# A fused attention and gated FFN kernel: instruction order from a stored table, FFN halves of 287 and 289 tokens, last output tile in two column halves

## The chip, the cores and the metric

The kernel runs on one core of a Trainium2 chip. The metric is the device time of one execution in microseconds; the median of several runs is compared. An execution is a little longer than the span from its first to its last instruction, which is what the profile shows.

## The reference

There are 8 batches, 8 heads, 576 tokens and a head width of 64, all in float32. The weights of the FFN come as float64 (`moe_w_in` 512 x 1024, `moe_conv_w` 3 x 1024, `moe_w_out` 1024 x 512), and the kernel decodes them from their two 32-bit words on the chip.

```python
scores = scale * np.matmul(q, k.transpose(0, 1, 3, 2))
mask = block_i >= block_j                      # blocks of 64 tokens
scores = np.where(mask, scores, -1000000000.0)
scores = scores - np.max(scores, axis=-1, keepdims=True)
attn = np.exp(scores)
attn = attn / (np.sum(attn, axis=-1, keepdims=True) + 1e-09)
x = (attn @ v).transpose(0, 2, 1, 3).reshape(B, S, H * D)
h = np.maximum(x @ w_in, 0.0)
conv_out = sum(conv_w[k] * hp[:, k:k + S] for k in range(3))   # hp: h with one zero token at each end
gate = 1.0 / (1.0 + np.exp(-conv_out))
return h * gate @ w_out
```

A token's gate needs the FFN's hidden value of the token before it and the one after it. A part of the tokens therefore needs one more column of `h` at each inner border.

## The kernel before, in words

**Precision.** TensorE works on 32-bit values in a reduced form. Each factor is split into a high and a low part, and products are sums of three matmuls: high by high, high by low, low by high. The parts are `wih`, `wil` for w_in, `woh`, `wol` for w_out, `xs[c][0]`, `xs[c][1]` for the attention's output, `gbuf[0]`, `gbuf[1]` for the gated hidden values.

**Attention.** Heads go in pairs, 4 pairs to a batch. For a pair, the q and k tiles are transposed on TensorE (`naturals`, L1020), evicted by ACT and DVE into high and low parts, and copied by DMA into stacked tiles (`mvz` L1057, `mv` L1077). `stage_s` computes scores block by block (L1227, L1229, L1182), DVE takes the maximum (L1237), ACT the exponential (L1240), POOL scales by the reciprocal sum (L1156). `stage_x` transposes the probabilities (L1418) and splits them by ACT and DVE (L1429, L1432, L1438). `stage_pv` multiplies them with v (L1516). `to_x` converts the pair's output on POOL to high and low parts (L675 and L1692), which the FFN reads.

**FFN.** `ffn(b, o0, o1, ...)` takes tokens o0 to o1 of a batch. For each of 8 blocks of 128 hidden units, 12 matmuls (4 chunks of 128 input features, 3 passes; L1598) fill one bank of PSUM, six planner operations of two matmuls each. ACT, DVE and POOL then apply the ReLU, the three taps of the convolution, the gate and the split (L1612 to L1638). For each output tile of 128 tokens, 24 matmuls of 512 columns follow (8 blocks, 3 passes; L1657), an eviction by ACT (L1667) and a store (L1670). Batch 0 goes in two parts, tokens 0 to 254 after a first round of attention over 256 tokens ("A") and the rest after a second round ("B"). Batches 1 to 7 go in two halves of 288 tokens. A half computes 290 columns: two more at the inner border, of which one is used. Tokens that don't fill an output tile are carried to the next part.

**Weights.** w_in comes in 8 blocks (`load_w_in`, block 0 in two halves), w_out in 8 (`load_w_out`, DMA L972). `split` and `decode` work on each: ACT takes the absolute value (L817), POOL or DVE clamps (L823; the tuple `S2P` lists the blocks that POOL clamps), DVE shifts and joins words (L828 to L851), ACT writes the high part (L886). The low part is made in a bank: minus the high part (L902), plus the low word's share (L905). For the blocks in the tuple `WPA`, a full-precision matmul also adds the value itself (L911) and ACT copies the result (L914); for the others DVE adds the value while it reads the bank (L908).

**Order.** The kernel isn't written in the order in which it runs. Each piece of work is handed to a planner as an operation with an engine, a duration, what it depends on, buffers and a due time (`Plan.op`). When all are known, `Plan.order` plans the whole program: `forward` goes through time, at each step takes the engine that can start first, and on it the ready operation with the earliest due time; FFN matmuls are marked `paced`, and are held back until they come within `WINDOW` (19.66 us) of the first attention operation not yet started. `late` then plans backwards to give new due times, and the two are repeated `ROUNDS` (24) times; the plan that ends first is kept. The resulting sequence on each engine is fixed in the program. DMA loads and stores are issued by SyncE (SP), one queue in order. The planner knows durations by formula (`c_act`, `c_dve`, `c_pool`, `mm_`), transfer times (`xfer`), a port that DVE and POOL share, the 8 banks of PSUM, and a clock of TensorE that falls after little use. In gaps of TensorE that it foresees, it puts dummy matmuls (`work`, L1808).

Of the kernel before, what the change touches and what calls it, by code (L numbers as in the profile page):

```python
# [18 lines left out]
PE, DVE, ACT, POOL, SP = 0, 1, 2, 3, 4  # L19

# [72 lines left out]
class Plan:  # L93
# [53 lines left out]

    def late(self, done):  # L150
        ops = self.ops
        top = max(o.end for o in ops)
        left = [0] * len(ops)
        for o in ops:
            for d in o.deps + o.after:
                left[d.seq] += 1
        rt = [0.0] * len(ops)
        free, port = [0.0] * 5, 0.0
        ready, future = [[] for _ in range(5)], [[] for _ in range(5)]
        for o in ops:  # L160
            if not left[o.seq]:
                heapq.heappush(future[o.eng], (0.0, top - o.end, o.seq, o))
        n = len(ops)
        res = [0.0] * n
        while n:
            best = None
            for e in range(5):
                t = free[e]
                while future[e] and future[e][0][0] <= t:
                    o = heapq.heappop(future[e])[3]  # L170
                    heapq.heappush(ready[e], (top - o.end, o.seq, o))
                if ready[e]:
                    p, _, o = ready[e][0]
                    cand = (max(t, port) if o.port else t, p, e, o, 0)
                elif future[e]:
                    t, p, _, o = future[e][0]
                    cand = (max(t, port) if o.port else t, p, e, o, 1)
                else:
                    continue
                if best is None or cand[:2] < best[:2]:  # L180
                    best = cand
            t, _, e, o, where = best
            heapq.heappop(future[e] if where else ready[e])
            end = t + (o.end - o.start)
            free[e] = end
            if o.port:
                port = end
            res[o.seq] = end
            n -= 1
            for d in o.deps + o.after:  # L190
                lat = self.DRAIN[d.eng] + (self.SIGNAL[e] if d.eng != e else 0.0) if (d.eng != PE or e != PE) else 0.0
                rt[d.seq] = max(rt[d.seq], end + d.lat + lat)
                left[d.seq] -= 1
                if not left[d.seq]:
                    heapq.heappush(future[d.eng], (rt[d.seq], top - d.end, d.seq, d))
        return [top - r for r in res]

    def order(self, window, skip, fill, clock, rounds, pair):
        best, least = None, 1e30
        for _ in range(rounds + 1):  # L200
            done = self.forward(window, skip, fill, clock, pair)
            if done is None:
                break
            end = max(o.end for o in self.ops)
            if end < least:
                best, least = done, end
                slots = [(b, b.slot) for q in self.queue.values() for b in q]
            for o, t in zip(self.ops, self.late(done)):
                o.target = t
            window = 1e9  # L210
        for b, z in slots:
            b.slot = z
        return best

    def forward(self, window, skip, fill, clock, pair):
# [22 lines left out]

        n = len(slots)
# [34 lines left out]
        front = sorted((o for o in self.ops if o.eng == PE and not o.paced), key=lambda o: (o.target, o.seq))  # L274
        fpos = 0
# [4 lines left out]
        open_, force = [], False  # L280
# [13 lines left out]
        while left:  # L294
            left -= 1
            best = None
            while fpos < len(front) and front[fpos].start is not None:
                fpos += 1
            limit = front[fpos].target + window if fpos < len(front) else 1e30
            for e in range(5):  # L300
                t = free[e]
                if e == PE:
# [3 lines left out]
                    for o in open_:  # L306
                        if o.paced and o.target > limit and not force:
                            continue
# [38 lines left out]
                if best is None or cand[:2] < best[:2]:  # L347
                    best = cand
            if best is None:
                if force:  # L350
                    return None
                force = True
                left += 1
                continue
            force = False
# [77 lines left out]
def kernel(  # L433
# [19 lines left out]
    HS = S // 2  # L453
    SCALE = 1.0 / 8.0
# [41 lines left out]
    S2P = tuple(range(16))  # L496
# [8 lines left out]
    WPA = (0, 1, 2, 3)  # L505
# [4 lines left out]
    WINDOW = 19.66  # L510
    ROUNDS = 24
# [136 lines left out]
    def c_pool(n, two_in=False):  # L648
        return 0.1 + n * 0.0022 if two_in else 0.16 + n / 1200.0
# [28 lines left out]
    def load_nat(p, at, part=None):  # L678
# [3 lines left out]
        for z, src in enumerate((q, k)):  # L682
# [10 lines left out]
            res.append((n, pl.op(SP, 1.5, go, at, bufs=ns[0:z + 1], xfer=c_dma(2 * (S - P * c0) * D * 4, 256))))  # L693
# [7 lines left out]
    def load_v(p, at, part, load_at=None):  # L701
# [11 lines left out]
        ld = pl.op(SP, 2.4, go, at if load_at is None else load_at, bufs=[vn], xfer=c_dma(2 * 5 * P * D * 4, 256))  # L713
# [99 lines left out]
    def decode(parts, scratch, deps, bufs, at, low=None, pool=False):  # L813
        fin, clamp = [], []
        for j, (words, n) in enumerate(parts):
# [3 lines left out]
            clamp.append(pl.op(ACT, c_act(n, False), s1, at, deps=deps, bufs=bufs))  # L819
# [12 lines left out]
        if pool:  # L832
            o3 = pl.op(POOL, c_pool(tot), s2, at, deps=clamp, bufs=bufs)
# [3 lines left out]
        for j, (words, n) in enumerate(parts):  # L837
# [19 lines left out]
            o4 = pl.op(DVE, c_dve(n), s4, at, deps=[o3], bufs=bufs, port=True)  # L857
            o = pl.op(DVE, c_dve(n, True), s5, at, deps=[o4], bufs=bufs, port=True)
            o = pl.op(DVE, c_dve(n), s6, at, deps=[o], bufs=bufs, port=True)
# [9 lines left out]
    def split(f, parts, src, hi, lo, scratch, deps, bufs, at, go, share=1):  # L869
# [51 lines left out]
        else:  # L921
            o1 = pl.op(ACT, c_act(n_), fh, at + 1, deps=[x[0] for x in o], bufs=bufs)
# [117 lines left out]
    def stage_t(nat, at):  # L1040
# [10 lines left out]
        for which in range(2):  # L1051
            t0 = at + 2.0 * which
            es = both[which]
            if which == 0:
                for o_, z, f_, n in ((0, 0, 0, S), (64, S + 64, 0, S - 64), (64, S, S - 64, 64)):
# [4 lines left out]
                    o = pl.op(SP, 0.65, mvz, t0 + (1.6 if n > 64 else 4.5), deps=es[0::2], bufs=[qh, t["qz"]], xfer=c_dma(n * 256, 2048))  # L1060
# [12 lines left out]
            for dst, o_, src, f_ in moves:  # L1073
# [5 lines left out]
                ready[dst in ("qb", "kb")].append(pl.op(SP, 0.65, mv, t0 + 1.5, deps=need, bufs=[src, t[dst]], xfer=c_dma(S * 256, 2048)))  # L1079
# [765 lines left out]
```

## Time and profile before

| what | value |
|---|---|
| time, median of 3 runs (lowest, highest) | 771.57 us (770.54, 771.87) |
| the profiled execution | 771.25 us |
| its span, first to last instruction | 769.5 us |
| mean granted TensorE clock | 0.996 |
| instructions | 17039 |
| busy share of PE, DVE, ACT, POOL | 98%, 82%, 80%, 57% |
| read from and written to HBM | 38.30 MB, 9.44 MB |

PE is TensorE's matmuls, PEld its weight loads, which overlap them; SPq is SyncE's queue of DMA issues. A matmul's end is modelled and its tail lies over the next one's start, so a stretch in which PE is busy all the time can still hold short delays between starts. A line such as L1598 is a line of the kernel before.

### The profile page before, as it was taken

The page shows a single profiled execution, that of the slowest core. Times are in us where ns is not written, and L with a number is a line of the kernel's source. Part 1 is how long each engine was busy: PE and PEld are TensorE (multiplying, and loading weights), DVE is VectorE, ACT ScalarE, POOL GpSimd, SP SyncE. Part 2 cuts the span into 40 slices and gives each one's busy share as a digit, 9 for nine tenths or more (in the row PEclk, how much of TensorE's full clock was granted, in tenths as well). Part 3 has the DMA queues.
Part 4 walks back from the last instruction along what each step waited for, and adds up shares of the span by engine and source line. Part 5 has one row for each costly group of instructions (what it writes and reads, how often), then busy time and mean ns, then how long its engine had stood idle before and what let it go on. Part 6 is the DMA issues. An engine that isn't in the chain of part 4 may idle for free.

```text
span 769.5 us, 17039 instructions
## 1 busy us (share of the span) xinstructions
PE 752.4 (98%) x5245; PEld 678.1 (88%) x5245; DVE 633.1 (82%) x1849; ACT 614.4 (80%) x1780; POOL 440.2 (57%) x664
## 2 busy tenths in 40 slices
PE   8889999999999999999999999999999999999998
PEld 5668879888989899998989889898999889898996
DVE  5898979988979879798988879798898888896540
ACT  5999978977979779797978879797887868786761
POOL 4556665676565557557565656557566643665421
PEclk9999999999999999999999999999999999999999
DMA  9823574567554554455455554555456363530001
GB/s 258 222 66 93 144 180 111 126 150 165 120 125 118 141 139 115 108 137 134 102 134 135 122 133 105 123 129 140 109 140 143 83 145 100 133 88 14 15 29 42
DMA packets 165839, 92.66 MB, mean 120 GB/s; under 512 B 135516, under 2 KB 142196, under 8 KB 165748
## 3 DMA queue, kind: packets, MB, share of 16 engines
q1 hardware_dynamic: 165204, 91.43, 48.9%
q8 instruction: 43, 0.70, 0.4%
q14 instruction: 48, 0.39, 0.2%
q10 hardware_dynamic: 544, 0.13, 0.1%
HBM read 38.30 MB, written 9.44 MB: 62 GB/s over the span
## 4 chain that ended last, share of the span: by engine, by line
PE 84%; ACT 6%; DVE 5%; DMA 2%; issue 1%; POOL 1%; SPq 0%; ACTq 0%; DVEq 0%
PE bank L1657 25%; PE bank L1598 25%; PE bank L1516 12%; PE bank L1418 6%; PE bank L1227 4%; PE bank L1229 4%; PE bank L1182 3%; PE bank L1020 2%; DMA ptbh<-in_k_dram 1%; DMA x<-in_moe_w_out_dram 1%; DVE ptbl L1432 1%; DVE st L1237 1%; DVE t L1619 1%; ACT ptbh L1429 1%; DVE xt L1539 1%
## 5 line engine op out<-in xcount | busy, mean ns | idle before, releaser
L1598 PE MATMUL bank<-x,wih 128*128 128x290 f32 (+2 forms) x1024 | 183.3, 300 | 1.5 <-ACT ptbl L1438 1.1
L1638 POOL TENSOR_TENSOR gl<-t,gh 128x288 fp32r<-128x288 f32 (+2 forms) x128 | 103.5, 812 | 108.8 <-ACT gh L1635 105.8
L1598 PEld LDWEIGHTS bank<-x,wih 128*128 128x128 f32 x1024 | 151.8, 189 | 4.5 <-ACT ptbl L1438 1.2
L1657 PE MATMUL bank<-woh,gh 128*128 128x512 f32 x288 | 117.1, 407 | 0.0
L1657 PE MATMUL bank<-woh,gl 128*128 128x512 f32 x288 | 113.6, 395 | 0.0
L1657 PE MATMUL bank<-wol,gh 128*128 128x512 f32 x288 | 113.5, 394 | 0.0
L1237 DVE TENSOR_REDUCE st<-bank 128x1 f32<-128x128 f32 (+1 forms) x224 | 106.5, 480 | 2.6
L1429 ACT ACTIVATE ptbh<-bank 128x384 fp32r<-128x384 f32 (+2 forms) x192 | 94.1, 504 | 14.9 <-PE bank L1418 14.2
L1432 DVE TENSOR_TENSOR ptbl<-bank,ptbh 128x512 fp32r<-128x512 f32 (+1 forms) x144 | 90.6, 632 | 6.6 <-ACT ptbh L1429 4.9
L1598 PE MATMUL bank<-x,wil 128*128 128x290 f32 (+2 forms) x512 | 94.3, 298 | 0.0
L1619 DVE SCALAR_TENSOR_TENSOR t<-bank,cw,t 128x288 f32<-128x288 f32 (+3 forms) x128 | 64.7, 506 | 23.2 <-ACT t L1615 21.7
L1598 PEld LDWEIGHTS bank<-x,wil 128*128 128x128 f32 x512 | 76.9, 189 | 0.5
L675 POOL TENSOR_SCALAR vv<-vn 128x320 fp32r<-128x320 f32 (+2 forms) x68 | 30.7, 454 | 73.5 <-PE bank L1516 43.0
L1229 PE MATMUL bank<-kl,qz 128*128 128x128 f32 (+1 forms) x224 | 72.3, 324 | 0.0
L1516 PE MATMUL bank<-ptbl,vv 128*64 128x320 f32 (+1 forms) x256 | 67.8, 313 | 0.0
L1615 ACT ACTIVATE t<-bank,cw 128x288 f32<-128x288 f32 (+2 forms) x128 | 63.9, 500 | 2.9 <-POOL gl L1638 0.8
L1623 DVE SCALAR_TENSOR_TENSOR t<-bank,cw,t 128x287 f32<-128x287 f32 (+3 forms) x128 | 64.6, 505 | 1.3
L1657 PEld LDWEIGHTS bank<-woh,gl 128*128 128x128 f32 x288 | 54.0, 188 | 12.8
L1635 ACT ACTIVATE gh<-t 128x288 fp32r<-128x288 f32 (+2 forms) x128 | 56.6, 445 | 8.8 <-DVE t L1631 8.6
L1628 ACT ACTIVATE t<-t 128x288 f32<-128x288 f32 (+2 forms) x128 | 56.8, 444 | 8.5 <-DVE t L1623 7.6
L1631 DVE SCALAR_TENSOR_TENSOR t<-t,bank 128x288 f32<-128x288 f32 (+2 forms) x128 | 56.8, 445 | 6.9 <-ACT t L1628 5.7
L1539 DVE TENSOR_TENSOR xt<-bank,xt 64x256 f32<-64x256 f32 (+1 forms) x112 | 51.5, 460 | 10.6 <-ACT xt L1536 6.9
(209 smaller groups left out, 2060.9 us busy)
## 6 DMA issues: line engine op xcount, KB each, us to landing
out_dram<-stage SPq DMA_DIRECT2D x36, 256.0 KB, 2.2
vn<-in_v_dram SPq DMA_DIRECT2D x64, 128.0 KB, 2.7
ka<-kh SPq DMA_DIRECT2D x56, 144.0 KB, 2.8
kb<-kh SPq DMA_DIRECT2D x56, 144.0 KB, 2.8
qnf<-in_q_dram SPq DMA_DIRECT2D x56, 128.0 KB, 2.6
knf<-in_k_dram SPq DMA_DIRECT2D x56, 128.0 KB, 2.8
x<-in_moe_w_out_dram SPq DMA_DIRECT2D x8, 512.0 KB, 3.8
qa<-qh SPq DMA_DIRECT2D x28, 144.0 KB, 2.4
```

Source lines behind the costliest of these rows:

```text
L1229: nc.tensor.matmul(sb.ap[:, 0:nk], qz.ap[:, z:z + 128], kl.ap[:, 0:nk], start=False, stop=True)
L1237: nc.vector.tensor_reduce(out=st.ap[:, i:i + 1], in_=sb.ap[:, 0:nk], op=ALU.max, axis=AX.X, negate=True)
L1429: nc.scalar.activation(out=hi(), in_=src(), func=AF.Copy)
L1432: nc.vector.tensor_tensor(out=lo(), in0=src(), in1=hi(), op=ALU.subtract)
L1516: nc.tensor.matmul(tb.ap[0:m, q0 - qa:qb - qa], vv.ap[:, chunk(c), w[ps_]], pm.ap[:, 128 * c + q0:128 * c + qb] if qa == 0 else pm.ap[:, c ...
L1539: nc.vector.tensor_tensor(out=xt.ap[o64:o64 + 64, qa:qb], in0=tb.ap[64:128, 0:n], in1=xt.ap[o64:o64 + 64, qa:qb], op=ALU.add)
L1598: nc.tensor.matmul(fb.ap[:, 0:n2], wt[:, c, fs], xs[c][xi].ap[:, x0:x0 + n2], start=(n + c - c0 == 0), stop=(n + c - c0 == 3 * NCC - 1))
L1615: nc.scalar.activation(out=t.ap[:, 0:no], in_=fb.ap[:, own:own + no], func=AF.Copy, scale=cw[:, NFC + f:NFC + f + 1])
L1619: nc.vector.scalar_tensor_tensor(out=t.ap[:, i0:no], in0=fb.ap[:, own + i0 - 1:own + no - 1], scalar=cw[:, f:f + 1], in1=t.ap[:, i0:no], o ...
L1623: nc.vector.scalar_tensor_tensor(out=t.ap[:, 0:i1], in0=fb.ap[:, own + 1:own + 1 + i1], scalar=cw[:, 2 * NFC + f:2 * NFC + f + 1], in1=t.a ...
L1638: nc.gpsimd.tensor_tensor(out=gbuf[1].ap[:, f, carry:carry + no], in0=t.ap[:, 0:no], in1=gbuf[0].ap[:, f, carry:carry + no], op=ALU.subtract)
L1657: nc.tensor.matmul(fb.ap[:, 0:DM], gbuf[a].ap[:, f, cs], w[:, f, :], start=(f == 0 and n == 0), stop=(f == NFC - 1 and n == 2))
```

## The change

The due times no longer come from backward planning. A table `TARGETS` holds one number for each of the 6,548 operations, in twentieths of a microsecond, and `order` makes one forward pass by it: `late`, the rounds and the window are gone. In that pass, when several engines could start at the same time, the shared port is no longer given by due time but to whoever comes first, and TensorE is looked at first. Many durations of the planner are edited; these change no instruction, only the order. The other edits change instructions:

- `S2P` loses block 0, whose clamp goes from POOL to DVE; `WPA` loses blocks 2 and 3, whose low part goes the way of L908.
- The six operations of an FFN block go chunk pair by chunk pair (chunks 0 and 1 in all three passes, then 2 and 3) instead of pass by pass.
- Batches 1 to 7 are parted at token 287 (`HF`), and a part takes one column more at each inner border: 0 to 287 computes 288 columns, 287 to 576 computes 290.
- The very last output tile is computed as two tiles of 256 columns, each with its 24 matmuls, its eviction and its store.

```diff
+TARGETS = """
+231 194 254 295 389 351 165 219 342 348 472 477 329 315 701 761 443 547 562 576 594 587 607 619 656 686 462 554 425 501 333 343 354 372 346 370 574 538 372
...
-    def order(self, window, skip, fill, clock, rounds, pair):
-        best, least = None, 1e30
-        for _ in range(rounds + 1):
-            done = self.forward(window, skip, fill, clock, pair)
...
-    def forward(self, window, skip, fill, clock, pair):
+    def order(self, targets, skip, fill, clock, pair):
...
+        assert len(targets) == len(self.ops)
+        for o, x in zip(self.ops, targets):
+            o.target = x / 20
...
-                        if o.paced and o.target > limit and not force:
-                            continue
...
-                        cand = (t if now else then[0][0], o.target, e, o, 2)
+                        cand = (t if now else then[0][0], -1.0, e, o, 2)
...
-                    cand = (max(t, port) if o.port else t, o.target, e, o, 1)
+                    cand = (max(t, port) if o.port else t, t, e, o, 1)
...
-                        cand = (t, b.target, e, b, 0)
+                        cand = (t, t, e, b, 0)
                     else:
-                        cand = (max(t, port) if late else t, a.target, e, a, 0)
+                        cand = (max(t, port) if late else t, t, e, a, 0)
...
-                moved = max(o.end + 1.2, moved) + o.xfer
+                moved = max(o.end + 1.2, moved) + o.xfer * (1.5 if moved < 4.5 else 1.0)
...
-                    z = min((max(freed[z], o.start), last[z] != b.tag, z) for z in range(n) if tenant[z] is None)[2]
+                    z = min((max(freed[z] + o.ldw, o.start), last[z] != b.tag, z) for z in range(n) if tenant[z] is None)[2]
...
+    HF = HS - 1
...
-    S2P = tuple(range(16))
+    S2P = tuple(range(1, 16))
...
-    WPA = (0, 1, 2, 3)
+    WPA = (0, 1)
...
-            res.append((n, pl.op(SP, 1.5, go, at, bufs=ns[0:z + 1], xfer=c_dma(2 * (S - P * c0) * D * 4, 256))))
+            res.append((n, pl.op(SP, 1.5, go, at, bufs=ns[0:z + 1], xfer=2 * (S - P * c0) * D * 4 / 160e3)))
...
-                ready[dst in ("qb", "kb")].append(pl.op(SP, 0.65, mv, t0 + 1.5, deps=need, bufs=[src, t[dst]], xfer=c_dma(S * 256, 2048)))
+                ready[dst in ("qb", "kb")].append(pl.op(SP, 0.65, mv, t0 + 1.5, deps=need, bufs=[src, t[dst]], xfer=S * 0.00128))
...
-        own = min(o0, 2 if o1 - o0 == HS else 1)
+        own = min(o0, 1)
         no = o1 - o0
         x0 = o0 - own
-        n2 = own + no + (0 if o1 == S else 2 if o1 - o0 == HS else 1)
+        n2 = own + no + int(o1 < S)
...
-            for wt, xi in ((wih, 0), (wil, 0), (wih, 1)):
-                for c0 in (0, 2):
+            for c0 in (0, 2):
+                for wt, xi in ((wih, 0), (wil, 0), (wih, 1)):
...
+            cut = DM // 2 if b == B - 1 and o1 == S and i == nt - 1 else DM
+            for d0 in range(0, DM, cut):
+                ds = slice(d0, d0 + cut)
+                if d0:
+                    fb = bank(TAIL2[0])
...
+                            nc.tensor.matmul(fb.ap[:, 0:cut], gbuf[a].ap[:, f, cs], w[:, f, ds], start=(f == 0 and n == 0),
+                                             stop=(f == NFC - 1 and n == 2))
...
+                    nc.scalar.activation(out=ob.ap[:, ds], in_=fb.ap[:, 0:cut], func=AF.Copy)
...
+                    nc.sync.dma_start(out=ofl[row:row + P, ds], in_=ob.ap[:, ds])
...
-                    for half in range(2):
-                        c = ffn(b, HS * half, HS * half + HS, xb, c, H * SLOT / 2)
+                    c = ffn(b, 0, HF, xb, c, H * SLOT / 2)
+                    ffn(b, HF, S, xb, c, H * SLOT / 2)
...
-    for o in pl.order(WINDOW, SKIP, (work, psum, (NBANK0, NBANK, TB), 0.234, LEAST, SPARE), CLOCK, ROUNDS, (NEAR, FAR, BIAS)):
+    for o in pl.order([int(x) for x in TARGETS.split()], SKIP, (work, psum, (NBANK0, NBANK, TB), 0.234, LEAST, SPARE), CLOCK, (NEAR, FAR, BIAS)):
```

More of the change, by code (lines that the diff above doesn't have):

```diff
@@ L145, in op @@
         return o
[L150 to L178, printed above, removed]
-                    continue
[L180 to L196, printed above, removed]
@@ L198, in order @@
-    def order(self, window, skip, fill, clock, rounds, pair):
-        best, least = None, 1e30
-        for _ in range(rounds + 1):
-            done = self.forward(window, skip, fill, clock, pair)
[L202 to L213, printed above, removed]
@@ L272, in forward @@
                 d.outs.append(o)
-        front = sorted((o for o in self.ops if o.eng == PE and not o.paced), key=lambda o: (o.target, o.seq))
-        fpos = 0
         free = [0.0] * 5
@@ L296, in forward @@
             best = None
-            while fpos < len(front) and front[fpos].start is not None:
-                fpos += 1
-            limit = front[fpos].target + window if fpos < len(front) else 1e30
             for e in range(5):
@@ L817, in s1 @@
                 nc.scalar.activation(out=scratch(j), in_=words(1).bitcast(F32), func=AF.Abs)
-            clamp.append(pl.op(ACT, c_act(n, False), s1, at, deps=deps, bufs=bufs))
+            clamp.append(pl.op(ACT, c_act(n, False) + 0.04, s1, at, deps=deps, bufs=bufs))
         def s2():
@@ L832, in decode @@
         if pool:
-            o3 = pl.op(POOL, c_pool(tot), s2, at, deps=clamp, bufs=bufs)
+            o3 = pl.op(POOL, c_pool(tot) + 0.03, s2, at, deps=clamp, bufs=bufs)
         else:
@@ L921, in split @@
         else:
-            o1 = pl.op(ACT, c_act(n_), fh, at + 1, deps=[x[0] for x in o], bufs=bufs)
+            o1 = pl.op(ACT, c_act(n_, False), fh, at + 1, deps=[x[0] for x in o], bufs=bufs)
         o2 = pl.op(PE, run(mm_(n_)), less, at + 1, deps=[o1], bufs=[fb])
@@ L1150, in i2 @@
             nc.vector.reciprocal(st.ap[:, a:b_], st.ap[:, a:b_])
-        o = pl.op(DVE, 0.15, i1, t0, deps=exps[4] if blocks[0] == 4 else [exps[x] for x in blocks], bufs=[st])
-        o = pl.op(DVE, 0.12, i2, t0, deps=[o], bufs=[st])
+        o = pl.op(DVE, 0.075, i1, t0, deps=exps[4] if blocks[0] == 4 else [exps[x] for x in blocks], bufs=[st])
+        o = pl.op(DVE, 0.09, i2, t0, deps=[o], bufs=[st])
         for x in blocks:
@@ L1245, in stage_s @@
             if not pmask:
-                o = pl.op(DVE, 0.07, mk, t0 + 0.3, deps=[o], bufs=[sb])
+                o = pl.op(DVE, 0.055, mk, t0 + 0.3, deps=[o], bufs=[sb])
             o = pl.op(DVE, c_dve(nk), mx, t0 + 0.3, deps=[o], bufs=[sb, st])
@@ L1652, in ffn @@
             cs = slice(i * P, (i + 1) * P)
-            o = None
-            for f in range(NFC):
-                def mm(f=f, fb=fb, cs=cs):
-                    for n, (a, w) in enumerate(((0, woh), (0, wol), (1, woh))):
-                        nc.tensor.matmul(fb.ap[:, 0:DM], gbuf[a].ap[:, f, cs], w[:, f, :], start=(f == 0 and n == 0),
-                                         stop=(f == NFC - 1 and n == 2))
-                o = pl.op(PE, run(*[mm_(DM)] * 3), mm, clock, deps=[o, gdone[f], wdone[NFC + f]], bufs=[fb], paced=True)
-                clock += 3 * mm_(DM)[0] * rate
@@ new lines, in ffn, with mm, ev, st @@
+            for d0 in range(0, DM, cut):
+                ds = slice(d0, d0 + cut)
+                if d0:
+                    fb = bank(TAIL2[0])
+                o = None
+                for f in range(NFC):
+                    def mm(f=f, fb=fb, cs=cs, ds=ds, cut=cut):
+                        for n, (a, w) in enumerate(((0, woh), (0, wol), (1, woh))):
+                            nc.tensor.matmul(fb.ap[:, 0:cut], gbuf[a].ap[:, f, cs], w[:, f, ds], start=(f == 0 and n == 0),
+                                             stop=(f == NFC - 1 and n == 2))
+                    o = pl.op(PE, run(*[mm_(cut)] * 3), mm, clock, deps=[o, gdone[f], wdone[NFC + f]], bufs=[fb], paced=True)
+                    clock += 3 * mm_(cut)[0] * rate
+                tail.append(o)
+                def ev(fb=fb, ob=ob, ds=ds, cut=cut):
+                    nc.scalar.activation(out=ob.ap[:, ds], in_=fb.ap[:, 0:cut], func=AF.Copy)
+                def st(ob=ob, row=row, ds=ds):
+                    nc.sync.dma_start(out=ofl[row:row + P, ds], in_=ob.ap[:, ds])
+                o = pl.op(ACT, c_act(cut), ev, clock, deps=[o], bufs=[fb, ob])
+                pl.op(SP, 0.5, st, clock + 1, deps=[o], bufs=[ob], xfer=c_dma(P * 4 * cut, 1024 if cut < DM else 2048))
```

38 lines of the change are left out of this document (11 added, 27 removed), and 222 rows, old and new, of the table TARGETS.

## The prediction

> **What bounds the kernel now.** I read the page first, then the busy time by stretch, then the waits, the chain and the last microseconds. The page has TensorE (PE) busy for nearly the whole span and on most of the chain.
>
> ```profile
> span 769.5 us, 17039 instructions
> PE 752.4 (98%) x5245; PEld 678.1 (88%) x5245; DVE 633.1 (82%) x1849; ACT 614.4 (80%) x1780; POOL 440.2 (57%) x664
> ...
> PE 84%; ACT 6%; DVE 5%; DMA 2%; issue 1%; POOL 1%; SPq 0%; ACTq 0%; DVEq 0%
> ```
>
> So another order can give back only what TensorE loses, and the next view says where that is. Its columns are the stretch, its length, the busy time of PE, weight loads, DVE, ACT and POOL with their instruction counts, the granted TensorE clock, and the DMA share and rate.
>
> ```profile
> core 0: us, PE busy (x) PEld busy (x) DVE busy (x) ACT busy (x) POOL busy (x), PEclk, DMA share, GB/s
> 0.00:20.00 20.00, 16.91 (x90) 11.20 (x90) 12.08 (x41) 12.24 (x37) 8.39 (x19) 1.00 0.92 260
> 20.00:40.00 20.00, 18.13 (x133) 12.62 (x133) 16.44 (x44) 19.76 (x62) 11.88 (x22) 1.00 0.78 202
> 40.00:60.00 20.00, 17.84 (x115) 14.04 (x115) 19.09 (x46) 18.38 (x50) 9.65 (x14) 0.93 0.27 68
> 60.00:80.00 20.00, 19.44 (x153) 16.24 (x153) 18.02 (x50) 18.79 (x55) 13.37 (x19) 0.98 0.46 115
> 80.00:100.00 20.00, 17.49 (x136) 14.99 (x134) 17.36 (x43) 17.95 (x50) 12.64 (x21) 1.00 0.52 135
> 100.00:120.00 20.00, 19.51 (x131) 17.88 (x131) 16.62 (x49) 15.89 (x45) 10.98 (x18) 0.91 0.73 167
> 120.00:140.00 20.00, 19.50 (x144) 18.05 (x143) 19.30 (x59) 17.61 (x53) 13.32 (x19) 1.00 0.59 139
> 140.00:160.00 20.00, 18.97 (x128) 16.47 (x127) 18.80 (x63) 17.51 (x55) 14.30 (x22) 1.00 0.50 115
> 160.00:200.00 40.00, 38.95 (x284) 35.28 (x283) 34.35 (x105) 31.12 (x90) 22.76 (x36) 1.00 0.70 158
> ...
> 200.00:700.00 500.00, 499.88 (x3567) 463.20 (x3567) 433.29 (x1298) 412.00 (x1213) 301.85 (x451) 1.00 0.51 121
> ```
>
> From 200 to 700 us TensorE idles 0.12 us in 500: nothing visible is left there. Before 200 us it idles 3.09 + 1.87 + 2.16 = 7.12 us in the first 60 and 0.56 + 2.51 + 0.49 + 0.50 + 1.03 + 1.05 = 6.14 us from 60 to 200. In 20 to 40 us ACT is busy 19.76 of 20, in 40 to 60 DVE 19.09 of 20: there the decoding of the weights on ACT and DVE is the bound, and order helps little. The clock is below 1 in two places. Stretches as long as a slow spell, each with the one ahead of it, show the pattern:
>
> ```profile
> 53.87:57.28 3.41, 2.08 (x16) 1.71 (x16) 3.35 (x8) 2.90 (x10) 0.61 (x1) 1.00 0.43 99
> 57.28:60.69 3.41, 3.41 (x18) 2.77 (x19) 2.83 (x8) 2.53 (x9) 0.73 (x1) 0.50 0.12 24
> 98.24:101.65 3.41, 1.64 (x11) 1.40 (x12) 1.40 (x5) 2.85 (x8) 2.70 (x5) 1.00 0.30 88
> 101.65:105.06 3.41, 3.41 (x15) 2.99 (x14) 1.94 (x6) 2.51 (x7) 0.95 (x2) 0.50 1.11 291
> ```
>
> After 3.41 us with TensorE busy only 2.08 or 1.64, the next 3.41 us ran at half clock. Each slow spell loses 1.7 us of work, 3.4 in all.
>
> The Trainium skill ("TensorE: Matmul & The Clock Gate", What's actually happening) has the clock fall after a window of about 3.4 us that was idle. The trace agrees on the length, but here a half-busy window was enough; by the page's wording neither spell would have come, and the term for the clock below would be nothing.
>
> What starved the second stretch stands in the chain (start, length, what) and in the waits of TensorE (total, times, longest):
>
> ```profile
> 91.36 6.74 DMA x<-in_moe_w_out_dram
> 98.62 1.80 DMA qz<-qh
> ```
>
> ```profile
> PE bank L1418 <- ACT ptbl L1438: 1.4, 1, 1.4
> PE bank L1598 <- ACT ptbl L1438: 1.1, 1, 1.1
> PE bank L1227 <- DMA qz<-qh: 0.5, 1, 0.5
> ```
>
> A load of w_out took 6.74 us, ACT stood behind it in its own order, and TensorE behind ACT; the query copy came late as well.
>
> **The change, part by part.** The sum is made against the profiled execution, 771.25 us: the span of 769.5 and 1.75 around it. The median of the runs is 771.57, 0.32 above, so the same difference is taken from that.
>
> *FFN parted at 287.* In batches 1 to 7 the first half multiplies 288 columns instead of 290; the second keeps 290. The widths of ACT, DVE and POOL move by one column, which changes nothing that I can price. The pitch comes from the undisturbed end of the chain:
>
> ```profile
> 712.00 12.94 PE bank L1598 x96
> ...
> 748.99 16.80 PE bank L1657 x72
> ```
>
> That is 134.8 ns for 290 columns and 233.3 ns for 512, so 0.44 ns a column. 7 x 8 x 12 = 672 matmuls lose two columns: **-0.6 us**, all on the path, since TensorE has no idle time there. Bounds 0 and -0.6.
>
> *Last tile in two halves.* 24 matmuls of 512 columns become 48 of 256 with twice the weight loads. Rows: the end of the kernel, a run of 256-column matmuls, a 256-column ACT read of a bank, and two transfers.
>
> ```profile
> 765.39 0.39 PE L1657 MATMUL bank<-woh,gl 128*128 128x512 f32 x1
> 765.87 0.60 ACT L1667 ACTIVATE stage<-bank 128x512 f32<-128x512 f32 x1 [5.05 <-PE bank L1657]
> 766.49 0.33 SPq L1670 DMA_DIRECT2D out_dram<-stage  x1
> ```
>
> ```profile
> 64.66 0.64 PE L1598 MATMUL bank<-x,wih 128*128 128x256 f32 x4
> 65.13 0.40 PE L1598 MATMUL bank<-x,wil 128*128 128x256 f32 x2
> ```
>
> ```profile
> L1612 ACT ACTIVATE bank<-bank 128x256 f32<-128x256 f32 x8 | 3.1, 391 | 0.3 <-PE bank L1598 0.2
> ```
>
> ```profile
> out_dram<-stage SPq DMA_DIRECT2D x36, 256.0 KB, 2.2
> ...
> qdl<-ql SPq DMA_DIRECT2D x56, 16.0 KB, 1.9
> ```
>
> Four 256-column matmuls, weight loads included, take 65.13 - 64.66 = 0.47 us, 118 ns each; two make 0.235 against 0.233, so TensorE's time stays. The first half's eviction and store run beside the 2.8 us of the second. After the last matmul the eviction takes 0.39 instead of 0.60, the store of 128 KB lies between 1.9 and 2.2 us, say -0.15, and the matmul itself ends about 0.1 sooner: **-0.45 us**, with bounds -0.6 and, if the second store waits behind the first one's issue, +0.3.
>
> A rule of the Trainium skill speaks against this part: "TensorE: Matmul & The Clock Gate", The mechanism, says that a weight load overlaps a running matmul only where the row groups differ, and LDWEIGHTS (loading the stationary operand) gives 107 ns for 128 columns. By that the 24 added loads would cost 2.6 us, and this part would be +2.1. The row of 118 ns, about what the columns alone take, contradicts it, so the sum goes without.
>
> *Decoding of w_in.* Blocks 2 and 3 take their low part with DVE's add from the bank, as 4 to 15 do, instead of a full-precision matmul and an ACT copy. Block 0 has its clamp on DVE instead of POOL.
>
> ```profile
> 24.31 0.86 PE bank L911 x2
> ```
>
> ```profile
> L911 PE MATMUL bank<-gl,ident 128*128 128x512 f32 x4 | 2.0, 590 | 0.0
> L908 DVE TENSOR_TENSOR wil<-bank,gl 128x512 fp32r<-128x512 f32 x2 | 1.4, 688 | 0.0
> ```
>
> TensorE loses four pieces of 0.43 us, 1.7 in all, and ACT two copies; DVE gains two adds of 0.69, in a stretch where it is busy 16.44 of 20. Since ACT is the full engine there, I take **-0.8 us**. Bounds: -1.7, all of TensorE's part on the path, and +1.4, both adds on it.
>
> *The table.* It issues nothing new, but places every instruction of every engine, the loads on SyncE's one queue too. The edited durations only steer the planner, above all those of transfers: a whole q or k load (294,912 bytes) goes from 1.38 to 1.84 us, a half-tile copy from 0.38 to 0.74. That is the error behind the late copy above. The window that held FFN work back to 19.66 us beyond the attention front is gone; the table alone decides. I price it in two pieces. **Idle time:** the 2.51 us of 80 to 100 and the 0.49 of 100 to 120 come from late transfers, so they should go, -3.0; of the first 60 us, bound by ACT and DVE, I take a tenth, -0.7. Together **-3.7**. The bounds are -11.6 (all idle time to 200 us but for the 1.6 us before the first matmul) and +6 (as much new idle time as 60 to 200 us has now). **Clock:** with the stall at 98 us goes the slow spell behind it, **-1.7**; the one at 57 us stands in DVE's full stretch and stays. Bounds -3.4 and, with two spells more, +3.4. The stalls removed leave ACT and DVE next, whose busy times are not shortened.
>
> *FFN order inside a bank.* The two first chunks now get all three passes before the others. The six later matmuls still wait for the last pair's data, and everything on TensorE's queue stands behind them. From 200 us on no such wait shows now, so this is taken at 0; the cost if that cover goes is the third rival.
>
> Sum: -0.6 - 0.45 - 0.8 - 3.7 - 1.7 = -7.25. The profiled execution would take 764.0 us, the median of runs **764.3 us**.
>
> **The rivals.** (1) *The stalls only move.* The durations of the planner are nearer but not exact, and 20 to 60 us is full on ACT and DVE. Then the fixed parts are left, -0.6 - 0.45 - 0.4 = -1.45, and it takes **770.1 us**. For it: losses already sit in one small stretch. Against: the largest has one named cause that the change corrects.
>
> (2) *The early part is truly repacked.* Nearly all 11.6 us of idle time, both slow spells (3.4) and the fixed 1.05 go: -16, **755.5 us**. For it: ACT has 7.8 idle us in the first 20, DVE 7.9, so decoding can begin sooner. Against: the loads fill 0.92 of the DMA engines in that stretch.
>
> (3) *FFN started too early: slower.* With the window gone, an FFN half of each of the seven later batches may start on chunks 0 and 1 before the last pair is converted, and the in-order TensorE then waits in the bank's middle. The conversion on POOL is the wait:
>
> ```profile
> L1692 POOL TENSOR_TENSOR x<-xt,x 128x576 fp32r<-128x576 f32 x28 | 40.1, 1433 | 1.3
> ...
> L675 POOL TENSOR_SCALAR x<-xt 128x576 fp32r<-128x576 f32 x28 | 19.0, 680 | 9.8 <-DVE xt L1539 8.7 <-PE bank L1598 0.8
> ```
>
> 1.43 + 0.68 = 2.1 us, seven times, is +14.8 on the forecast, **779.1 us** in full. It decides from 1.3 us a batch, where -7.25 + 8.8 passes +0.2%. For it: the accumulation now can start on half the data. Against: TensorE idles 0.12 us in 500, and priorities would have to misjudge every batch.
>
> **How the numbers follow.** About 0.2%, 1.5 us, is what a measurement of this kernel can tell from no change. Forecast (759 to 768) 0.55; rival 2 0.17; rival 1 0.14; rival 3 0.14. Faster: 0.55 + 0.17 + 0.05 of rival 1 = 0.77. Within: 0.07 of rival 1 and 0.01 of a mild rival 3 = 0.08. Slower: 0.02 of rival 1 and 0.13 of rival 3 = 0.15. The range reaches down to rival 2, 755, and up to a rival 3 just past its point, 774; the forecast's own is 759 to 768.
>
> **What would show it.** Right: 80 to 100 us has TensorE busy over 19.5 and no DMA of several us in the chain; one clock figure below 1 at most before 110 us; FFN matmuls of 288 columns; an eviction near 0.39 at the end. Wrong: TensorE idle time from 200 us on above 2 us (rival 3), early idle time still near 13 us (rival 1), or under 5 (rival 2). A 256-column pitch in the last tile well over 118 ns would overturn the second part, and a gain spread over 200 to 700 us would mean that the idle times were the wrong place to look.

## The result, and the profile after

The changed kernel takes 759.0 us (median of 4 runs, 758.09 to 759.42), the kernel before 771.06 us in the same comparison (4 runs). The ratio is 0.984, with a 95% interval of 0.982 to 0.986: 12.1 us faster, where 7.25 were forecast. In a second comparison the two gave 759.65 and 770.16 us, a ratio of 0.986 (0.983 to 0.988). The profiled executions are 759.42 and 771.25 us, their spans 757.6 and 769.5.

The page of the kernel after, its head and the chain by engine:

```profile
span 757.6 us, 17060 instructions
PE 746.9 (99%) x5278; PEld 678.4 (90%) x5278; DVE 630.8 (83%) x1853; ACT 613.8 (81%) x1779; POOL 437.5 (58%) x662
...
PE 91%; ACT 3%; DVE 2%; DMA 2%; SPq 1%; issue 1%; ACTq 0%; DVEq 0%
```

TensorE's share of the chain went from 84 to 91%. The same stretches as before (PE, weight loads, DVE, ACT, POOL, clock, DMA):

```profile
0.00:20.00 20.00, 16.35 (x84) 11.51 (x85) 12.13 (x39) 12.03 (x31) 8.11 (x18) 1.00 0.96 252
20.00:40.00 20.00, 17.94 (x137) 13.11 (x137) 17.43 (x51) 19.25 (x64) 11.80 (x20) 1.00 0.78 210
40.00:60.00 20.00, 18.77 (x134) 14.66 (x135) 17.78 (x46) 19.45 (x56) 9.20 (x15) 1.00 0.29 71
60.00:80.00 20.00, 19.72 (x166) 17.71 (x165) 19.05 (x52) 19.55 (x57) 14.82 (x24) 1.00 0.47 119
80.00:100.00 20.00, 20.00 (x147) 17.19 (x147) 18.88 (x51) 19.35 (x54) 13.29 (x21) 1.00 0.71 175
100.00:120.00 20.00, 20.00 (x150) 18.82 (x149) 19.44 (x59) 16.68 (x48) 11.79 (x18) 1.00 0.78 163
...
160.00:200.00 40.00, 39.63 (x297) 36.91 (x295) 36.32 (x118) 34.19 (x105) 24.55 (x39) 1.00 0.64 151
200.00:700.00 500.00, 499.96 (x3550) 462.17 (x3550) 428.20 (x1277) 408.37 (x1193) 299.20 (x448) 1.00 0.50 120
```

The first 60 us idle 3.65 + 2.06 + 1.23 = 6.94 us, against 7.12: that part did not gain, though 37 dummy matmuls stand in it instead of 24. From 60 to 160 us, 5.1 us of idle time became 0.4. The stretch of 80 to 100 us is full, with 175 GB/s moved in it instead of 135, and the chain has no load in it; behind its first 12 us the only DMA of several us in the chain is a store, 4.09 us from 172.97.

No slow spell of the clock shows. This profile holds no clock record at all, so its 1.00 is no measurement; the second profile of the same kernel has records from 6.38 us on and none of half clock up to 757 us, and the work counted below runs alike in both.

Idle time isn't all, since dummy matmuls count as busy and a matmul's tail covers a short delay. So I also added up the work that TensorE had started by a given time, from all its rows. It is an estimate: 2 ns plus 0.4545 ns a column for each matmul, close to the 133.4 ns for 288 and 233.3 ns for 512 columns in the rows (half of the share by column for the paired 64-row ones, 0.43 us for a full-precision piece of 512 columns), dummies not counted. In us of work:

```text
by time (us)        60     100     160     200     700    all  last matmul starts
before             31.5    62.7   113.9   149.9   624.0  689.5  765.39
after              30.5    65.7   121.4   157.7   632.7  687.2  754.32
after, 2nd profile 31.6    66.9   122.4   157.5   632.3  687.2  754.61
```

The second profile of the same kernel agrees within 1.2 us. The kernel after is 1.0 us behind at 60 us, where it has spent some 3 us on 13 more dummies; from 60 to 160 us it gains 8.5, and at 200 us it has 7.8 us more work behind it. From 200 to 700 it adds 0.9. It also has 2.3 us less to do. These make the 11.07 us between the starts of the last matmuls, and the end behind them, shorter by 0.75, makes the rest.

### The profile page after: what moved, and what is told of

Same layout as the page of the kernel before. It is cut to its first block, busy times and chain, and to the rows that moved or that the text cites. A ratio compares the mean times of both kernels' runs of the same rounds, so it can differ in the third digit from the quotient of the medians.

```text
span 757.6 us, 17060 instructions
## 1 busy us (share of the span) xinstructions
PE 746.9 (99%) x5278; PEld 678.4 (90%) x5278; DVE 630.8 (83%) x1853; ACT 613.8 (81%) x1779; POOL 437.5 (58%) x662
## 4 chain that ended last, share of the span: by engine, by line
PE 91%; ACT 3%; DVE 2%; DMA 2%; SPq 1%; issue 1%; ACTq 0%; DVEq 0%
PE bank L1744 28%; PE bank L1810 26%; PE bank L1662 13%; PE bank L1564 7%; PE bank L1375 5%; PE bank L1373 4%; PE bank L1328 3%; PE bank L1166 2%; DMA gh<-in_moe_w_in_dram 1%; PE bank L1419 1%; DMA out_dram<-stage 1%; PE bank L1581 0%; DMA ptbh<-in_k_dram 0%; DVE st L1496 0%; ACT p1f L1504 0%
## 5 line engine op out<-in xcount | busy, mean ns | idle before, releaser
L1744 PE MATMUL bank<-x,wih 128*128 128x290 f32 (+3 forms) x1024 | 199.5, 300 | 0.3 <-ACT stage L1818 0.3
L1784 POOL TENSOR_TENSOR gl<-t,gh 128x289 fp32r<-128x289 f32 (+3 forms) x128 | 103.2, 809 | 124.0 <-ACT gh L1781 116.9
L1810 PE MATMUL bank<-woh,gh 128*128 128x512 f32 (+1 forms) x296 | 119.3, 403 | 0.0
L1810 PE MATMUL bank<-woh,gl 128*128 128x512 f32 (+1 forms) x296 | 115.0, 389 | 0.0
L1810 PE MATMUL bank<-wol,gh 128*128 128x512 f32 (+1 forms) x296 | 114.9, 388 | 0.0
L1744 PE MATMUL bank<-x,wil 128*128 128x290 f32 (+3 forms) x512 | 110.3, 298 | 0.0
L1765 DVE SCALAR_TENSOR_TENSOR t<-bank,cw,t 128x289 f32<-128x289 f32 (+3 forms) x128 | 65.1, 509 | 22.8 <-ACT t L1761 21.8
L1761 ACT ACTIVATE t<-bank,cw 128x289 f32<-128x289 f32 (+3 forms) x128 | 63.7, 499 | 2.2 <-POOL gl L1784 0.3
L1774 ACT ACTIVATE t<-t 128x289 f32<-128x289 f32 (+3 forms) x128 | 56.8, 445 | 10.3 <-DVE t L1769 9.2
L1777 DVE SCALAR_TENSOR_TENSOR t<-t,bank 128x289 f32<-128x289 f32 (+3 forms) x128 | 57.0, 446 | 5.9 <-ACT t L1774 4.7
```

The lines of the kernel that those rows point to most:

```text
L1744: nc.tensor.matmul(fb.ap[:, 0:n2], wt[:, c, fs], xs[c][xi].ap[:, x0:x0 + n2], start=(n + c - c0 == 0), stop=(n + c - c0 == 3 * NCC - 1))
L1761: nc.scalar.activation(out=t.ap[:, 0:no], in_=fb.ap[:, own:own + no], func=AF.Copy, scale=cw[:, NFC + f:NFC + f + 1])
L1765: nc.vector.scalar_tensor_tensor(out=t.ap[:, i0:no], in0=fb.ap[:, own + i0 - 1:own + no - 1], scalar=cw[:, f:f + 1], in1=t.ap[:, i0:no], o ...
L1777: nc.vector.scalar_tensor_tensor(out=t.ap[:, 0:no], in0=t.ap[:, 0:no], scalar=1.0, in1=fb.ap[:, own:own + no], op0=ALU.add, op1=ALU.mult)
L1784: nc.gpsimd.tensor_tensor(out=gbuf[1].ap[:, f, carry:carry + no], in0=t.ap[:, 0:no], in1=gbuf[0].ap[:, f, carry:carry + no], op=ALU.subtract)
L1810: nc.tensor.matmul(fb.ap[:, 0:cut], gbuf[a].ap[:, f, cs], w[:, f, ds], start=(f == 0 and n == 0), stop=(f == NFC - 1 and n == 2))
```

## The experiments

Three theories were set against each other. **A:** the gain comes from right durations, above all of transfers. **B:** it comes from the order that the search found. **C:** it comes from the edited instructions. Ratios are to the kernel before on the same chip; the kernel after has 0.984 and 0.986 by that measure, 759.0 and 759.65 us.

| run | median us | ratio (95%) |
|---|---|---|
| before, new durations alone | 766.67 | 0.996 (0.994 to 0.997) |
| all but the table | 765.59 | 0.994 (0.993 to 0.996) |
| after, old durations | 763.00 | 0.991 (0.990 to 0.993) |
| before, late loads halved | 766.96 | 0.996 (0.995 to 0.998) |
| after, 290 columns | 759.18 | 0.986 (0.981 to 0.991) |
| after, last tile whole | 758.95 | 0.985 (0.982 to 0.989) |
| after, old decoding | 762.28 | 0.989 (0.986 to 0.993) |
| after, no dummies | 762.05 | 0.989 (0.985 to 0.992) |
| after, pass by pass | 762.62 | 0.992 (0.990 to 0.994) |
| after, early due times shaken | 764.57 | 0.995 (0.993 to 0.998) |
| after, late due times shaken | 762.45 | 0.992 (0.990 to 0.994) |
| after, again | 759.65 | 0.986 (0.983 to 0.988) |

**New durations alone.** All edits of durations and nothing else; of them, for example:

```diff
-            res.append((n, pl.op(SP, 1.5, go, at, bufs=ns[0:z + 1], xfer=c_dma(2 * (S - P * c0) * D * 4, 256))))
+            res.append((n, pl.op(SP, 1.5, go, at, bufs=ns[0:z + 1], xfer=2 * (S - P * c0) * D * 4 / 160e3)))
```

> The kernel before with the planner's edited durations alone (transfers, ACT, DVE and POOL formulas); its instructions, backward planning and 24 rounds stay. Theory A, the gain comes from transfers that the planner now times rightly: the stall of 80 to 105 us and the slow clock behind it go, 765 to 768 us. Theory B, it comes from the order that the search found, of which right durations are only the condition: within 1.5 us of the kernel before, 769.6 to 772.6. Theory C, it comes from the edited instructions: the same as B here.

It came out at 0.996, 3.3 us faster by the ratio, and at 766.67 us inside the range of theory A. The stretches of 80 to 100 and 100 to 120 us:

```profile
80.00:100.00 20.00, 19.67 (x142) 16.78 (x141) 18.40 (x46) 19.24 (x52) 15.25 (x23) 1.00 0.61 149
100.00:120.00 20.00, 20.00 (x150) 18.58 (x149) 18.48 (x54) 16.61 (x49) 12.49 (x20) 1.00 0.60 138
```

The 3.0 us of idle time there are 0.33 now. With the new durations the old planner avoids the stall, as the step of the prediction that laid it to mistimed transfers has it. The run edits the durations of ACT, DVE and POOL along with those of transfers and doesn't set them apart; the halved loads below do point to transfers. And it is only a quarter of the gain.

**All but the table.** The kernel after, with due times from the old backward planning and its 24 rounds:

```diff
-    for o in pl.order([int(x) for x in TARGETS.split()], SKIP, (work, psum, (NBANK0, NBANK, TB), 0.234, LEAST, SPARE), CLOCK, (NEAR, FAR, BIAS)):
+    for o in pl.order(WINDOW, SKIP, (work, psum, (NBANK0, NBANK, TB), 0.234, LEAST, SPARE), CLOCK, ROUNDS, (NEAR, FAR, BIAS)):
```

> Everything of the change but the table: edited durations, first-come port, edited instructions, with due times from the old backward planning in 24 rounds. Theory A: 760 to 763 us, the table adds 1 to 4. Theory B: 765 us or more, the table adds 6 or more. Theory C: within 1.5 us of the kernel after, 757.5 to 760.5.

0.994, so the table itself brings the step from 0.994 to 0.984 or 0.986, some 6 to 8 us: theory B for the larger part. Against the new durations alone, on the same chip, the edited instructions and the port rule brought about 1 us (766.67 to 765.59), which the two intervals don't tell from nothing; theory C finds no support here. Its view by stage is instructive:

```profile
0.00:60.00 60.00, 53.38 (x333) 39.69 (x335) 44.56 (x123) 46.47 (x136) 30.97 (x51) 0.94 0.65 175
60.00:160.00 100.00, 98.86 (x738) 88.86 (x734) 95.41 (x271) 90.14 (x260) 65.88 (x100) 1.00 0.57 139
160.00:200.00 40.00, 39.92 (x294) 36.81 (x293) 37.02 (x116) 34.19 (x103) 23.35 (x37) 1.00 0.67 158
200.00:700.00 500.00, 499.21 (x3554) 461.03 (x3553) 429.83 (x1293) 410.20 (x1205) 302.23 (x453) 1.00 0.50 120
```

TensorE idles 6.62 + 1.14 + 0.08 = 7.84 us before 200, as little as in the kernel after (7.67). The difference hides in what counts as busy: 49 dummy matmuls instead of 37 (2.8 us), the clock at 0.94 in the first 60 us, and delays between starts. By work, it stands at 116.0 us by 160 (after: 121.4) and at 625.3 by 700 (632.7).

**The table with the old durations** in its forward pass, the edits of the first experiment reversed:

```diff
-            res.append((n, pl.op(SP, 1.5, go, at, bufs=ns[0:z + 1], xfer=2 * (S - P * c0) * D * 4 / 160e3)))
+            res.append((n, pl.op(SP, 1.5, go, at, bufs=ns[0:z + 1], xfer=c_dma(2 * (S - P * c0) * D * 4, 256))))
```

> The kernel after, its table too, with the old durations in the one forward pass. Theory A: transfers are mistimed again and the stalls come back, 764 to 768 us. Theory B: the table holds the order and the durations matter little once it is there, 759 to 761. Theory C: 759 to 760.

763.0 us lies between the two theories, 3.4 to 4 above the kernel after.

```profile
60.00:160.00 100.00, 97.75 (x722) 87.20 (x720) 93.93 (x271) 89.46 (x259) 65.25 (x100) 1.00 0.59 140
```

2.25 us idle instead of 0.36 between 60 and 160 us: the table needs the durations that it was made with.

**The late load.** The kernel before, its compute in exactly the same order, with the second half of the last three w_out blocks left out:

```diff
-        def go(raw=raw, src=src):
-            nc.sync.dma_start(out=raw.ap.rearrange("p n w -> p (n w)"), in_=src.bitcast(I32))
+        def go(raw=raw, src=src, m=512 if f > 4 else 1024):
+            nc.sync.dma_start(out=raw.ap.rearrange("p n w -> p (n w)")[:, 0:m], in_=src.bitcast(I32)[:, 0:m])
```

> The kernel before, in exactly its order, with the loads of the w_out blocks 5, 6 and 7 cut to their first half (256 KB instead of 512; the other half of these blocks is left out, so part of the output is not the reference's). If the late load at 91 us starves ACT and then TensorE: idle time of TensorE from 80 to 120 us falls from 3.0 to under 1, the slow clock at 101.6 to 105.1 us does not come, 766.5 to 768.5 us. If the load only ends a wait that another cause would end later: 770 to 772 us, the slow clock stays.

0.996, 2.5 to 3 us faster, and

```profile
80.00:100.00 20.00, 18.72 (x145) 16.43 (x142) 18.41 (x47) 19.04 (x53) 13.67 (x23) 1.00 0.51 133
100.00:120.00 20.00, 20.00 (x147) 18.32 (x146) 19.20 (x59) 16.04 (x46) 11.15 (x17) 1.00 0.72 164
```

1.28 us idle instead of 3.00, a little more than expected. Of TensorE's three waits in the prediction, the one of L1598 for ACT, 1.1 us, is still there; its cause stays open. The ratio shows that these loads were a cause of the stall and not only the end of another wait. The stretches are less clean, since this execution ran about 2 us ahead before the first of the three loads was issued. The slow spell at 101.6 us is gone, but in this profile the one at 57.3 us is missing too, which the edit can't have touched; whether a spell comes also differs between executions of one order. Over all runs of this comparison the mean granted clock was 0.9964 for the kernel before (13 runs) and 0.9984 here (10).

**290 columns again** in the first halves, plan and order kept:

```diff
-        n2 = own + no + int(o1 < S)
+        n2 = own + no + int(o1 < S); nw = n2 + 2 * (o1 == HF)
...
-                            nc.tensor.matmul(fb.ap[:, 0:n2], wt[:, c, fs], xs[c][xi].ap[:, x0:x0 + n2],
+                            nc.tensor.matmul(fb.ap[:, 0:nw], wt[:, c, fs], xs[c][xi].ap[:, x0:x0 + nw],
```

> The kernel after, in exactly its order, with 290 instead of 288 columns in the matmuls of the first FFN halves of batches 1 to 7 (the two more columns are computed and not used). All theories: +0.6 us, and a start-to-start time of these 672 matmuls of about 134.8 instead of 133.9 ns. If the two columns lie in delays that something else sets: no difference.

759.18 us: a time can't tell 0.6 us here. The rows can. First and last piece of an unbroken run of 80 such matmuls, here and in the second profile of the kernel after:

```profile
702.88 0.98 PE L1744 MATMUL bank<-x,wih 128*128 128x290 f32 x6
...
713.13 0.70 PE L1744 MATMUL bank<-x,wih 128*128 128x290 f32 x4
```

```profile
703.19 0.96 PE L1744 MATMUL bank<-x,wih 128*128 128x288 f32 x6
...
713.33 0.70 PE L1744 MATMUL bank<-x,wih 128*128 128x288 f32 x4
```

76 starts apart: 134.9 against 133.4 ns. Over all neighbours of these widths after 200 us that start less than 170 ns apart, the means are 134.5 and 133.4. That is 1.1 ns, 0.7 us for 672 matmuls.

**The last tile whole,** the ten due times of its second half left out of the table:

```diff
-            cut = DM // 2 if b == B - 1 and o1 == S and i == nt - 1 else DM
+            cut = DM
```

> The kernel after, in its order, with the last output tile in one piece of 512 columns. From the two traces: the time from the start of the last matmul to the end of the span goes from 3.28 back to 4.1 us, so +0.8 us. By the prediction's sum +0.45.

758.95 us, again inside the noise, but the ends can be laid side by side. Whole, then in halves (the kernel after), and the store of a half:

```profile
752.67 0.39 PE L1810 MATMUL bank<-woh,gl 128*128 128x512 f32 x1
```

```profile
753.15 0.60 ACT L1818 ACTIVATE stage<-bank 128x512 f32<-128x512 f32 x1 [5.05 <-PE bank L1810]
```

```profile
754.32 0.28 PE L1810 MATMUL bank<-woh,gl 128*128 128x256 f32 x1
```

```profile
754.63 0.38 ACT L1818 ACTIVATE stage<-bank 128x256 f32<-128x256 f32 x1 [2.37 <-PE bank L1810]
```

```profile
out_dram<-stage SPq DMA_DIRECT2D x2, 128.0 KB, 1.7
```

From the last matmul's start to the end of the span it is 4.08 us whole and 3.33 in halves: 0.17 by an earlier eviction, 0.22 by a shorter one, the rest by the store.

**The old decoding of w_in:**

```diff
-    S2P = tuple(range(1, 16))
+    S2P = tuple(range(16))
...
-    WPA = (0, 1)
+    WPA = (0, 1, 2, 3)
```

> The kernel after with the decoding of w_in as before: block 0 clamped on POOL, blocks 2 and 3 with the full-precision matmul and ACT's copy. The added matmul takes the due time of the one before it; all other due times stay. Theories A and B: +0.8 us, 0 to +1.7. Theory C: +2.5 or more.

762.28 us, some 3 us slower, what theory C asked for; the two runs above, within the same comparison, take 759.18 and 758.95. But it isn't a clean price of the decoding. Its plan has six dummies more than the kernel after (43 to 37), 1.4 us, and the next three runs show the same: the table was made for the other instructions, and whatever moves it costs about as much.

**Pass by pass:**

```diff
-            for c0 in (0, 2):
-                for wt, xi in ((wih, 0), (wil, 0), (wih, 1)):
+            for wt, xi in ((wih, 0), (wil, 0), (wih, 1)):
+                for c0 in (0, 2):
```

> The kernel after with the six operations of an FFN block pass by pass as before; the table's due times go to the six in turn. Theories A and B: within 1 us. Theory C, the chunk order lets the FFN begin before the last pair is ready and so gives TensorE work: +2 us or more, with new idle time of TensorE from 200 us on. If the prediction's third rival holds any truth (the chunk order makes TensorE wait in the middle of a bank), it is faster.

762.62 us, about 3 us slower, with 0.26 us of idle time from 200 to 700 us. So the chunk order does not make TensorE wait in the middle of a bank; the third rival is out. About half of the loss stands in one place, hidden in a busy stretch, beside POOL's conversion of the last pair:

```profile
704.24 1.78 PE L1959 MATMUL bank<-rident 128*128 128x512 f32 x7
```

```profile
704.41 1.43 POOL L1843 TENSOR_TENSOR x<-xt,x 128x576 fp32r<-128x576 f32 x1
```

Seven dummies fill a gap that the planner foresaw, about 1.6 us; in the kernel after, FFN matmuls on chunks 0 and 1 run while POOL converts. Yet the kernel before, pass by pass too, has no dummy after 36 us: its order has matmuls of an output tile (L1657) there. So this half is a table that doesn't fit the other chunk order, and not the price of that order. The rest stays open.

**Due times shaken** by up to 0.5 us, before 160 us (`x < 3200`) or from there on (`x >= 3200`):

```diff
-    for o in pl.order([int(x) for x in TARGETS.split()], SKIP,
+    for o in pl.order([x + ((i * 7919 + x * 104729) % 21 - 10) * (x < 3200) for i, x in enumerate(map(int, TARGETS.split()))], SKIP,
```

> The kernel after with every due time below 160 us shifted by a made-up amount of up to 0.5 us either way; the later ones stay. Theory A, the rough order and right durations are what counts: +0 to +1.5 us. Theory B, the fine order is what the search found: +3 us or more, with TensorE idle or slow-clock time back in the first 200 us.

> The kernel after with every due time from 160 us on shifted by a made-up amount of up to 0.5 us either way; the earlier ones stay. All theories that put the gain before 200 us: +0 to +1.5 us, TensorE idle from 200 to 700 us stays under 1. If the fine order also matters where TensorE is full: +2 us or more.

Early: 764.57 us, 5 slower, as theory B has it. Late: 762.45, 3 slower, where every theory expected at most 1.5. These two and the pass-by-pass run were compared with the kernel before alone, which took 768.81 us there, 1 to 2 less than beside the kernel after; the kernel after did not run with them. By the ratios the losses are larger: 7 to 8.5 us early, 5 to 6 late, 5 to 6 pass by pass.

With the early ones shaken, TensorE idles 7.64 us before 200 us, no more than in the kernel after (7.67); but 51 dummies stand in it instead of 37 (3.3 us), and the clock is at 0.92 in the first 60 us of this profile. Six of its ten executions have a mean clock of 1.000 and still take 763.1 to 764.6 us. The kernel with the late ones shaken, from 200 to 700 us:

```profile
200.00:700.00 500.00, 499.37 (x3530) 459.63 (x3530) 427.52 (x1276) 408.56 (x1189) 297.58 (x445) 1.00 0.50 120
```

TensorE idles 0.63 us there, and still does 2.8 us less work than in the kernel after (472.2 against 475.0 us; its second profile has 474.8). So a stretch that reads as fully busy holds delays that a fine order can make longer or shorter. Up to half a microsecond either way on single due times takes back a quarter of the gain (late, by times) to two thirds (early, by ratios).

**No dummy matmuls,** all else in order:

```diff
-            for _ in range(k):
+            for _ in range(0):
```

> The kernel after, in exactly its order, without the 37 dummy matmuls of the first 40 us. If a window in which TensorE is half busy is enough for the half clock, as in the kernel before: several stretches of 3.4 us at half clock in the first 60 us, and +1 to +4 us. If the clock falls only after idle windows: at most the first stretch, before the first real matmul, is slow, and within 1 us of the kernel after.

762.05 us, some 2.5 to 3 slower, with one slow spell; its stretch and the one ahead of it:

```profile
27.99:31.40 3.41, 1.84 (x13) 1.39 (x13) 3.12 (x11) 3.41 (x15) 0.31 (x1) 1.00 1.15 255
31.40:38.23 6.83, 6.83 (x40) 5.46 (x41) 4.39 (x11) 4.93 (x16) 4.52 (x7) 0.50 0.50 131
```

Again the window ahead of the spell was half busy, 1.84 of 3.41 us, and not idle. The loss has two parts that the rows show: the clock comes up later (last section), and 6.83 us run at half clock.

**The kernel after again,** unchanged, as an anchor on one more chip:

> The kernel after, unchanged, beside the kernel before, as the anchor for the other runs. If the difference between the chips is small: 758 to 760 us. Where the kernel before has a mean clock near 0.997 here, and the kernel after 1.0, the ratio is 0.984 to 0.988.

759.65 us, as expected. One of its four executions has a mean clock of 0.995, and takes 759.80.

## Why the prediction was right, and where it was off

The direction and the place were right: the idle time of 60 to 160 us and the slow spells. The size was short by 4.85 us, and 759.0 lies at the lower edge of the forecast's own 759 to 768. Most of that is two terms rightly placed and taken too small, idle time (by 1.9) and clock (by 1.7). The terms below overlap and need not add up, since dummies count as busy. Step by step:

- **FFN at 287:** -0.6 forecast, -0.7 by the starts of neighbouring matmuls. Right.
- **Last tile:** -0.45 forecast, -0.75 by the two ends. The mis-sized parts are the store, 1.7 us for 128 KB, below the 1.9 that the prediction took as the lowest, and the eviction, which began 0.17 us sooner. The pitch of 256 columns is 117 ns in the last tile, where 118 was foreseen.
- **Decoding:** -0.8 forecast. The 1.7 us of TensorE's work are gone; the time that they are worth by themselves isn't settled by the run above.
- **Idle time:** -3.7 forecast, 13.26 to 7.67 us in the profiles, -5.6. The piece from late transfers, -3.0, came as forecast, and two runs bear it out in part: the new durations took away 2.7 of it, the halved loads 1.7. The tenth of the first 60 us, -0.7, was -0.2: there the rows of ACT and DVE were the bound, as the prediction said itself, and ACT is at 19.25 and 19.45 of 20 after. What was missing are the smaller idle pieces of 60 to 80 and of 120 to 200 us, 3.1 us together, of which the new order removed 2.4.
- **Clock:** -1.7 forecast, on the ground that the spell at 57 us stays. Both went, -3.4 between the profiles. The better number is over executions: a mean clock of 0.9964 is 0.0036 x 770 = 2.8 us lost on average. They are rarer now and not abolished: of 16 executions with the start of the kernel after (it, its repeat, 290 columns, tile whole), three have a mean clock of 0.995 or 0.996. The ground that the prediction gave, that a half-busy window is enough, is too simple; the last section has the windows against it.
- **Delays inside busy stretches:** a step that failed. "From 200 to 700 us TensorE idles 0.12 us in 500: nothing visible is left there" was true and was used as if nothing were left. The kernel after does 0.9 us more work there (0.7 by its second profile), and one shaken order 2.8 less. The bounds of the table's term had no entry for this.
- **The window:** the prediction wrote that the table does away with the window of 19.66 us. In the code of before the window holds in the first of 25 passes alone (`window = 1e9` after it), so less was removed than the third rival supposed; the pass-by-pass run went against that rival too.

Rival 1 (the stalls only move) is out: 7.67 us of idle time, not 13. Rival 2, 755.5 us, lies 3.5 us from the result and the forecast 5.3, but its mechanism, an early start repacked, didn't happen: the first 60 us idle as before, and by 60 us no more work was done. Its size came from the clock and from 60 to 160 us.

## What to carry to other kernels

Where an engine reads 98% busy, count the work that it has started by a given time, without dummies, before saying what an order can still bring; busy time hides dummies, a slow clock and delays between starts. A planner's order is worth what its durations are worth: correcting them alone gave 3.3 us, and a table made with one set lost 3.4 to 4 us with another. An order tuned this far is brittle: what moved it, other instructions or a shake of up to half a microsecond, cost 3 to 5 us by times, while two edits that left it alone (290 columns, the last tile whole) cost nothing that a time can tell. So such a table is made last, and a part of a kernel can't be priced by undoing it under a table that was made with it.

## What the runs showed of the hardware

The clock starts low, and the view by stretch doesn't say so. Ahead of the first record it shows 1.00, yet the first dummies of the kernel before ran at half the later rate; the other two rows are one and the same pair of matmuls, in the kernel after and in it without dummies:

```profile
1.62 4.61 PE L1808 MATMUL bank<-rident 128*128 128x512 f32 x10 [1.62 <-DVE rident L657]
```

```profile
13.75 1.02 PE L1057 MATMUL bank<-gh,ident 128*128 128x512 f32 x2
```

```profile
14.79 1.91 PE L1057 MATMUL bank<-gh,ident 128*128 128x512 f32 x2
```

0.46 us a dummy, against 0.233 us later for 512 columns. In the two profiles of the kernel after, the single dummies start 0.43 us apart up to 5.5 and 6.3 us, and 0.23 to 0.24 apart from there: the clock came up 4.4 and 5.3 us after the first dummy. With dummies it is up at 13.75 us, without them not yet at 14.79, and the kernel lost 2.5 to 3 us.

The Trainium skill ("TensorE: Matmul & The Clock Gate", What's actually happening) has the low clock as the default, released after about 3.4 us of activity in a window that doesn't start with the kernel; the low start agrees, and so does a release that is later than 3.4 us and not the same in two executions. The free-running window also fits that one order showed slow spells at 57 and 101 us in one profile and none up to 80 us in another. That only an idle window brings the clock down again does not agree: windows with TensorE busy 2.08, 1.64 and 1.84 of 3.41 us came right before slow spells.

But a half-busy window is not the rule either. Stretches of the same length, each with the next one, from the new durations alone and from the early due times shaken, each on the 3.41 us grid of the spells in its own trace (the second is 13 steps behind the end of one at 60.46):

```profile
39.94:43.35 3.41, 2.86 (x14) 1.53 (x14) 3.38 (x11) 3.36 (x12) 1.45 (x2) 1.00 0.22 50
43.35:46.76 3.41, 3.41 (x17) 2.70 (x18) 2.41 (x9) 2.71 (x7) 2.59 (x4) 0.50 0.22 49
```

```profile
104.83:108.24 3.41, 1.82 (x17) 1.40 (x16) 2.71 (x7) 2.53 (x9) 0.82 (x3) 1.00 0.81 216
108.24:111.66 3.42, 3.42 (x27) 3.02 (x26) 2.51 (x10) 3.05 (x9) 0.79 (x2) 1.00 1.03 165
```

The first was busy for 2.86 us and the clock fell; the second for 1.82, and it did not. The share that the profile counts as busy doesn't decide alone, and what does stays open.
